# Gated linear attention and a mixer block on one core: the up product as three float32r products of 12-bit halves, with fewer buffers and a new order

## The chip, the cores and the metric

The kernel runs on one core of a Trainium2 chip. The metric is the device time of one execution in microseconds (us), the median of the runs shown. TensorE (PE) multiplies, with its weight loads shown apart as PEld; VectorE (DVE) and ScalarE (ACT) do everything between the products; GpSimd (POOL) and SyncE (SP) mostly issue transfers.

## The reference

An attention block with a complex gate feeds a mixer block. Four batches, eight heads, 768 steps, head size 48, so a model width of 384; the mixer widens to 1536.

```python
# attention, per batch and head: a complex state S (48 x 48)
mag = sqrt(a_re**2 + a_im**2); scale = minimum(mag, 0.999) / (mag + 1e-6)
for t in range(768):
    S = (a_re + 1j*a_im)[t, :, None] * scale * S + outer(k[t], v[t])
    y[t] = q[t] @ S.real
# mixer, per batch, x of 768 x 384 (heads side by side)
u = x + ((x.T @ U) @ V).T            # U: 768 x 32, V: 32 x 768
out = u + maximum(u @ w_ch1, 0.0) @ w_ch2   # 384 x 1536, 1536 x 384
```

All is float32, apart from U, V, w_ch1 and w_ch2, which arrive as float64.

## The kernel before

**Tiling.** Time is cut into 24 chunks of 128 steps, six a batch. Attention goes chunk by chunk: `gates` (L651) makes magnitudes and angles for groups of two chunks, `prep` (L849) weighs q and k and transposes them, `chain` (L883) forms the products inside the chunk and carries the 48x48 states. The mixer goes by pairs of chunks: 12 pairs, m = 0 to 11, three a batch. It can begin only when a batch's six chunks are through, because `rank` (L992, matmuls on L995) sums over all 768 steps. Then, per pair: `spread` (L1028) and `mixed` (L1041) make u from x, `turned` (L1046) transposes it into uT, an up product gives h = max(u w1, 0) in 12 blocks of 128 rows, and a down product (`down` for pair 0, `down_two` for pairs 1 to 8, `down_three` for 9 to 11; matmuls on L1270, L1313 and L1484) brings it back to 384 columns. Results leave from `leave` and `out_at`.

**The up product.** Pair 0 is multiplied ahead of its batch's rank term and corrected later. Pair 1 uses `up` (L1067): 36 float32 matmuls 128x128x256 (L1074). Pairs 2 to 11 use `up_fewer` (L1130): the 3x3 by 3x2 block product by 15 block products instead of 18. `combine` (L1221, its sums on L1234) forms eight mixed blocks of w1 once, at pair 2; `put` (L1152, sums on L1153) forms twelve mixed blocks of uT in nine DVE instructions a pair; `chain` inside it (L1174) runs 15 steps of four float32 matmuls 128x128x128 (L1181), and each step's result is copied (six times, ACT, L1189) or added on (nine times, DVE, L1193 or the helper `add`, L465). A float32 matmul shows as two records, a float32r one as one.

**Buffers.** The uT tile has two buffers, h one. QKC (weighed q or k) has three, QK (transposed q and k) three, AT two, GM two. `gate` holds six planes: x, y and two each of the real and imaginary gate. `extra` holds h of pair 0 and later mixed blocks. VP holds three chunks of v. `stage` takes the raw float64 weights, which `single` (L583) turns into float32 in w1 and w2.

**Order.** Nothing is issued as the code stands. Each operation is added to a plan with an engine, a cost, and what it reads, writes and takes: `PE`, `ACT`, `DVE`, `POOL`, `SP` (L434 to L446). Operations are numbered as they are added. `Plan.order` (L152) then issues them in the sequence of the long constant `ORDER`, checking only that needs and buffers allow it; since each engine runs its instructions in the sequence in which they are issued, `ORDER` is the schedule of every engine and queue. `SPARE` puts idle matmuls in front of a few operations to keep TensorE's clock up. Most work goes through small helpers, so that many groups of the profile share a line: `mul` (L462), `add` (L465), `act` (L459), `bounded` (L468).

float32r is already in use: from group 3 on, `split` (L732) cuts the gate's logarithms into a float32r part and a remainder, and `within` and `angles` (L747, L811) multiply each by the prefix matrix, two float32r matmuls with 384 columns a chunk:

```python
for u in range(2):
    nc.tensor.matmul(out=get(*ps), lhsT=prefix_r, rhs=of(("gs%d" % u, g), i), start=(u == 0), stop=(u == 1))
```

Of the kernel before, what the change touches and what calls it, by code (L numbers as in the profile page):

```python
# [24 lines left out]
GC = 2  # L25
# [91 lines left out]
)  # L117

SPARE = {
    122: 2, 132: 10, 193: 14, 217: 5,  # L120
}

DUMP = None
# [195 lines left out]
def kernel(  # L319
# [230 lines left out]
    for n in range(3):  # L550
        VP.append(singles.tile([128, H, D], FP, name="VP%d" % n))
# [1156 lines left out]
```

## Time and profile before

| | |
|---|---|
| median of three runs | 535.81 us (535.58 to 535.88) |
| span of the profiled execution | 533.9 us (a time of its own beside the span isn't recorded for it) |
| PE busy / PEld busy | 514.2 us (96%) / 468.1 us (88%) |
| DVE busy | 438.2 us (82%), 863 instructions |
| ACT busy | 295.8 us (55%), 531 instructions |
| POOL busy | 30.5 us (6%) |
| moved by DMA | 39.95 MB, mostly in the first half |
| granted TensorE clock | full |

How to read it: the span runs from the first to the last instruction of the program; the median also holds what lies around it. A busy share is an average over stages. PE's busy time takes in the modelled ends of pipelined matmuls, so that short gaps vanish in it. In a group's row stand line, engine, operation, out<-in, shape and count, then the busy time of the group and the mean of one in ns, then the idle time in front of it with what ended it. In the chain of waits a row is a start in us, a length in us, and what ran.

### The profile page before, as it was taken

The numbers are of one execution on the slowest core, as the hardware profiler recorded it, in microseconds if no ns is written. First come the engines' busy times: TensorE is split into PE (matmuls) and PEld (weight loads), VectorE is DVE, ScalarE is ACT, GpSimd is POOL, SyncE is SP. The second block draws the span as 40 slices with busy tenths as digits, with TensorE's granted clock in tenths as the row PEclk, the third lists the DMA queues.
The fourth block names the chain that finished last, engine by engine and source line by source line (L and its number), as shares of the span: only waits on it lengthen the run. The fifth ranks groups of instructions, "written<-read, shape, count | busy, mean of one in ns | idle before, by whom it ended". The sixth has DMA issues, their size and how long they took to land.

```text
span 533.9 us, 17164 instructions
## 1 busy us (share of the span) xinstructions
PE 514.2 (96%) x7494; PEld 468.1 (88%) x7494; DVE 438.2 (82%) x863; ACT 295.8 (55%) x531; POOL 30.5 (6%) x58
## 2 busy tenths in 40 slices
PE   2899999999999999999999999999999999999996
PEld 1777786757989989999999999999999999999996
DVE  7898988999999998897886887786878866877842
ACT  5889998893776866546647655543555412221000
POOL 1000000001020001001100001100010000000010
PEclk9999999999999999999999999999999999999999
DMA  9967985565233423601534150500240000000002
GB/s 226 206 114 194 191 145 163 171 107 112 41 75 92 63 46 80 111 1 29 118 53 83 33 106 25 98 9 23 47 70 26 2 2 1 1 2 1 1 28 97
DMA packets 150706, 39.95 MB, mean 75 GB/s; under 512 B 145880, under 2 KB 147440, under 8 KB 150624
## 3 DMA queue, kind: packets, MB, share of 16 engines
q1 hardware_dynamic: 148544, 34.63, 32.3%
q0 software_dynamic: 2080, 4.15, 2.3%
q8 instruction: 61, 1.00, 0.8%
q14 instruction: 21, 0.17, 0.1%
HBM read 33.60 MB, written 4.76 MB: 72 GB/s over the span
## 4 chain that ended last, share of the span: by engine, by line
PE 81%; DVE 11%; ACT 3%; issue 2%; DMA 2%; SPq 0%; DVEq 0%; ACTq 0%
PE down L1313 20%; PE few L1181 13%; PE bank L1181 12%; PE bank L1484 7%; PE bank L872 4%; PE bank L901 4%; PE up L1074 3%; PE bank L959 3%; PE bank L921 3%; PE bank L951 2%; DVE QKC L462 2%; PE bank L1036 1%; PE bank L747 1%; PE bank L751 1%; PE bank L811 1%
## 5 line engine op out<-in xcount | busy, mean ns | idle before, releaser
L878 ACT COPY QK<-bank 112x512 f32<-112x512 f32 x96 | 51.8, 591 | 18.2 <-PE bank L872 17.9
L1313 PE MATMUL down<-w,h 128*128 128x192 f32 x288 | 53.6, 331 | 0.0
L462 DVE TENSOR_TENSOR QKC<-qk,cs 128x768 f32<-128x768 f32 x48 | 45.0, 951 | 4.9 <-ACT cs L459 4.7
L459 ACT ACTIVATE gate<-gate 128x768 f32<-128x768 f32 (+1 forms) x50 | 39.8, 798 | 16.3 <-DVE wide L719 12.7
L1313 PEld LDWEIGHTS down<-w,h 128*128 128x128 f32 x288 | 47.0, 190 | 0.9
L465 DVE TENSOR_TENSOR xo<-bank,xo 128x192 f32<-128x192 f32 x78 | 25.3, 350 | 24.9 <-PE bank L1484 16.0
L1189 ACT COPY h<-few 128x512 f32<-128x512 f32 x35 | 20.3, 585 | 30.0 <-PE few L1181 29.9
L1074 PE MATMUL up<-uT,w 128*128 128x256 f32 x144 | 34.0, 385 | 0.2
L456 ACT ACT_TABLE_LOAD x24 | 30.8, 1283 | 1.1 <-PEq L1692 0.7
L1074 PEld LDWEIGHTS up<-uT,w 128*128 128x128 f32 x144 | 26.6, 190 | 5.0 <-DVE xo L465 0.5
L1181 PE MATMUL bank<-extra,w 128*128 128x128 f32 x232 | 30.3, 276 | 0.0
L872 PE MATMUL bank<-ident,QKC 64*112 64x64 f32 x768 | 29.1, 221 | 1.0 <-DVE G L468 0.4
L872 PEld LDWEIGHTS bank<-ident,QKC 64*112 64x112 f32 x768 | 24.4, 130 | 6.2 <-DVE QKC L462 1.4
L459 ACT ACTIVATE es<-bank 128x384 f32<-128x384 f32 x48 | 20.3, 495 | 16.6 <-PE bank L747 15.8
L797 POOL DMA_DIRECT2D gate<-F x15 | 12.5, 832 | 285.2 <-DVE F L820 167.2
L1181 PEld LDWEIGHTS bank<-extra,w 128*128 128x128 f32 x232 | 28.3, 192 | 0.1
L1313 PE MATMUL down<-stage 128*128 128x192 f32 x144 | 28.0, 332 | 0.2 <-DVE xo L465 0.2
L465 DVE TENSOR_TENSOR xo<-down,xo 128x192 f32<-128x192 f32 (+1 forms) x58 | 22.0, 386 | 7.1 <-PE down L1313 6.9
L901 PE MATMUL bank<-QK 112*64 112x64 f32 x768 | 26.6, 224 | 0.0
L901 PEld LDWEIGHTS bank<-QK 112*64 112x64 f32 x768 | 24.2, 138 | 1.3 <-issue 0.5
L459 ACT ACTIVATE cs<-F 128x384 f32<-128x384 f32 x48 | 23.3, 516 | 3.0 <-DVE F L820 2.9
L1313 PEld LDWEIGHTS down<-stage 128*128 128x128 f32 x144 | 23.5, 190 | 1.2 <-DVE xo L465 0.5
(249 smaller groups left out, 1228.6 us busy)
## 6 DMA issues: line engine op xcount, KB each, us to landing
stage<-in_moe_w_ch_dram SPq DMA_DIRECT2D x12, 768.0 KB
gate<-in_a_re_dram SPq DMA_DIRECT2D x24, 192.0 KB
gate<-in_a_im_dram SPq DMA_DIRECT2D x24, 192.0 KB
qk<-in_q_dram SPq DMA_DIRECT2D x24, 192.0 KB
qk<-in_k_dram SPq DMA_DIRECT2D x24, 192.0 KB
VP<-in_v_dram SPq DMA_DIRECT2D x24, 192.0 KB
out_dram<-xo POOLq DMA_DIRECT2D x13, 192.0 KB, 2.9
out_dram<-xo POOLq DMA_DIRECT2D x16, 96.0 KB, 2.5
```

The source lines that it names most:

```text
L456: ACT(1.4, rank, lambda: nc.scalar.preload_act_table_set(name), writes=[TABLE])
L459: return nc.scalar.activation(out=o, in_=i, func=f, **kw)
L462: nc.vector.tensor_tensor(out=o, in0=a, in1=b, op=OP.mult)
L465: nc.vector.tensor_tensor(out=o, in0=a, in1=b, op=OP.add)
L872: nc.tensor.transpose(out=get(*ps[r])[0:DQ, h], in_=get(*qkc)[at, h].rearrange("p u d -> p (u d)")[:, 0:DQ], identity=ident[at, at], tile_ ...
L878: nc.scalar.copy(out=get(*QK)[0:DQ, u].rearrange("p (h t) -> p h t", t=CH)[:, :, r * HC:(r + 1) * HC], in_=get(*ps[r])[0:DQ])
L901: nc.tensor.matmul(out=get(*ps0)[r:r + HC, h], lhsT=k_of(h, r, HC), rhs=q_of(h, r, HC), start=True, stop=True, tile_position=(0, r))
L1074: nc.tensor.matmul(out=get(*ps)[:, e], lhsT=w1[:, f, (ff + e) * 128:(ff + e + 1) * 128], rhs=get(*uT)[:, f], start=(f == 0), stop=(f == KD ...
L1181: nc.tensor.matmul(out=get(*ps)[:, q], lhsT=w()[:, q * 128:(q + 1) * 128], rhs=v[0](), start=(n == 0 and q == 0), stop=True, skip_group_ch ...
L1189: ACT(c_act(n3 * CH) - 0.045, RU, lambda i=i, k=k: nc.scalar.copy(out=at(i, k), in_=get(*ps)), [ps], [o])
L1313: nc.tensor.matmul(out=get(*to)[:, part], lhsT=x(j), rhs=y[:, j], start=(first and j == 0), stop=(j == KH - 1), skip_group_check=not first)
L1484: nc.tensor.matmul(out=get(*ps), lhsT=w[0]()[:, q], rhs=x[0]()[:, q], start=(n == 0 and q == 0), stop=(q == k3 - 1), skip_group_check=True)
```

## The change

The up product of pairs 1 to 11 becomes three float32r products. Each value is cut at a bit mask (0xFFFFF000) into a high part and a remainder. With wh, uh the high parts, wl the remainder of w1 times 2^12, ul the remainder of u, wd = wl - wh and ud = uh/2^12 - ul, the product is (wh uh + wl ul)(1 + 2^-12) + wd ud. The first two sum in one PSUM bank, the third goes to another; ACT copies the first with the factor, DVE adds the third and clips at zero. `up_fewer`, `combine` and their helpers go. Pair 0 keeps its float32 product.

```diff
+def cut_weights():                     # once, at pair 1
+    for f in range(KD):                # KD = 3
+        for y in range(2):             # halves of 768 columns
+            DVE: t  = w1 & CUT
+            DVE: w1 = w1 - t           # in place
+            ACT: wl = w1 * SHIFT       # float32r
+            DVE: wd = wl - t           # float32r
+        for y in range(2):
+            ACT: wh = copy of t        # float32r, in w1's place
```

That is the function with its arguments left out; the parts for each pair are in the kernel's own words:

```diff
@@ turned(), pairs 1 to 11
+            for r in range(2):
+                DVE(c_one(MC * KD * HC), R0, lambda r=r: nc.vector.tensor_scalar(
+                    out=top.bitcast(U32), in0=get(*tr[r]).bitcast(U32), scalar1=CUT, scalar2=None, op0=OP.bitwise_and), [tr[r]], [("low", 0)])
+                ACT(c_act(MC * KD * HC) - 0.045, R0, lambda r=r: nc.scalar.copy(out=half(get(*uh), r), in_=mixed_of(top)), [("low", 0)], [uh + (r,)])
+                DVE(c_dve(MC * KD * HC), R0, lambda r=r: nc.vector.tensor_tensor(
+                    out=half(get(*ul), r), in0=mixed_of(get(*tr[r])), in1=half(get(*uh).bitcast(FP), r), op=OP.subtract), [tr[r], uh + (r,)], [ul + (r,)])
+            DVE(c_dve(KD * N), R0, lambda: nc.vector.scalar_tensor_tensor(
+                out=get(*ud), in0=get(*uh).bitcast(FP), scalar=1.0 / SHIFT, in1=get(*ul).bitcast(FP), op0=OP.mult, op1=OP.subtract), [uh, ul], [ud])
@@ up_cut(ff), six times a pair
+            def sums(e):
+                for f in range(KD):
+                    nc.tensor.matmul(out=get(*X)[:, e], lhsT=get("wh", f)[:, at(e)], rhs=get(*uh)[:, f], start=(f == 0), stop=False)
+                for f in range(KD):
+                    nc.tensor.matmul(out=get(*X)[:, e], lhsT=wl_of(f)[:, at(e)], rhs=get(*ul)[:, f], start=False, stop=(f == KD - 1))
+            def crosses():
+                for e in range(2):
+                    for f in range(KD):
+                        nc.tensor.matmul(out=get(*Y)[:, e], lhsT=wd[:, f, at(e)], rhs=get(*ud)[:, f], start=(f == 0), stop=(f == KD - 1))
...
+            ACT(c_act(2 * N) - 0.045, R0, lambda: act(where_(), get(*X), AF.Copy, scale=1.0 + 1.0 / SHIFT), [X], [part] + own)
+            DVE(c_dve(2 * N), R0, lambda: nc.vector._custom_dve(
+                dve_ops.TENSOR_ADD_SAT, out=where_(), in0=get(*Y), in1=where_(), s0=math.inf, s1=0.0), [Y, part], done)
@@ buffers
-    w1 = singles.tile([128, KD, FF], FP, name="w1")
+    wd = singles.tile([128, KD, FF], FR, name="wd")
+    wl = singles.tile([128, KD - 1, FF], FR, name="wl")
+    for f in range(KD):
+        buffer(("w1", f), "w1_%d" % f, 1, [128, FF])
-    GL = [singles.tile([128, GC * DM], FP, name="GL")]
-    GS = [[singles.tile([128, GC * DM], FR, name="GS%d" % n)] for n in range(2)]
+    GS = [[singles.tile([128, GC * DM], FR, name="GS0")]]
-    GATE = singles.tile([128, 6, GC * DM], FP, name="gate")
+    GATE = singles.tile([128, 3, GC * DM], FP, name="gate")
-    extra = singles.tile([128, 2 * FF3 + 2 * H * CH], FP, name="extra")
+    NQ, NA, NM, NK = 2, 1, 1, 2
@@ squares of group 0's first chunk
-            ACT(c_act(2 * W) + 0.04, R1, squares, AR + AI, [X] + Y)
+            ACT(ca, R1, lambda: act(t(x), t(ar), AF.Square), AR, [X])
+            DVE(cd, R1, lambda: mul(t(y), t(ai), t(ai)), AI, Y)
@@ ORDER
-    91, 93, 95, 99, 96, 97, 101, 92, 112, 94, 113, 114, 98, 102, 103, 115, 116, 117, 0, 104, 105, 118, 119, 120, 3, 109, 110, 106, 121, 111, 107, 122,
+    92, 113, 95, 114, 115, 2206, 94, 116, 0, 93, 91, 3, 96, 97, 117, 98, 99, 5, 1, 11, 189, 190, 213, 2, 214, 147, 148, 118, 4, 102, 103, 104, 100,
...
```

So QKC has two buffers instead of three (NQ), AT one instead of two (NA), GM one instead of two (NM), QK two instead of three (NK). The second gate planes live in a pool of two planes whose place the third row block of wl (`wl2`) takes once groups 0 to 2 are done. y, the remainder of the split magnitudes and the scaled angle share one buffer; the split angle's remainder shares GL. uh, ul and ud of a pair take the three buffers of the uT tag, so one pair's halves stand there at a time. h of pair 0 goes to the h buffer. For pairs 10 and 11, thirds of h that found place in the third QK buffer go to the values' tile and to `stage`. `ORDER` is made anew in all its 2208 operations (2207 before), and `SPARE` follows the new numbers.

More of the change, by code (lines that the diff above doesn't have):

```diff
@@ L681, in magnitudes_of @@
                 return
-            def squares():
-                at, n = slice((lo - first) * DM, (hi - first) * DM), 4 if g < SINGLE and g % 2 else 2
-                act(GATE[:, 0:2, at], GATE[:, n:n + 2, at], AF.Square)
-            ACT(c_act(2 * W) + 0.04, R1, squares, AR + AI, [X] + Y)
+            ACT(ca, R1, lambda: act(t(x), t(ar), AF.Square), AR, [X])
+            DVE(cd, R1, lambda: mul(t(y), t(ai), t(ai)), AI, Y)
             DVE(cd, R1, lambda: nc.vector._custom_dve(dve_ops.TENSOR_ADD_SAT, out=t(l), in0=t(x), in1=t(y), s0=M2HI, s1=M2LO), [X] + Y, [L])
@@ L733, in split @@
             if g in SPLIT:
-                for u in range(2):
-                    ring(("gs%d" % u, g), "gs%d" % u, GS[u])
+                ring(("gs0", g), "gs0", GS[0])
+                buffer(("gs1", g), "gy", 1, [128, GC * DM], dtype=FR)
                 a, b = ("gs0", g), ("gs1", g)
@@ L841, in gates, with wl2 @@
         return magnitudes, totals, turns, waves
+    def wl2():
+        if ("wl2",) not in T:
+            T["wl2",] = pools["second"].tile([128, FF], FR, tag="second", name="wl2")
+        return T["wl2",]
     def T_of(i):
@@ L983, in out_of @@
         def out_of(nm, k, shape, padded):
-            late = nm == "uTp" and i0 >= (B - 1) * NCH + MC
-            psum((nm, k), "M" if nm in ("up", "down") or late or (nm, k) == ("rank", 0) else "T", shape, padded)
+            psum((nm, k), "M" if nm in ("up", "down") or (nm, k) == ("rank", 0) else "T", shape, padded)
             return nm, k
@@ L1037, in products @@
                                          rhs=get(*r)[at], start=True, stop=True, tile_position=(n * R, 0))
-            PE(0.45, R0, products, [r, ("V", 0)] + [uT + ("kept",)] * (m >= AHEAD), ps, way=4, steps=4 * NP)
+            PE(0.45, R0, products, [r, ("V", 0)], ps, way=4, steps=4 * NP)
             return ps
@@ L1057, in turned, with keep @@
             PE(0.39, R0, turn, us, tr, way=5, steps=2 * KD * MC)
-            for r in range(2):
-                def keep(copy, r=r):
-                    copy(out=get(*uT).rearrange("p f (c s t) -> p s c f t", c=MC, t=HC)[:, r],
-                         in_=get(*tr[r]).rearrange("p (c f) t -> p c f t", c=MC))
-                if r:
-                    ACT(c_act(MC * KD * HC) - 0.045, R0, lambda keep=keep: keep(nc.scalar.copy), [tr[r]], [uT + (r,)])
-                else:
-                    DVE(c_dve(MC * KD * HC), R0, lambda keep=keep: keep(nc.vector.tensor_copy), [tr[r]], [uT + (r,)])
+            if ahead:
+                for r in range(2):
+                    def keep(copy, r=r):
+                        copy(out=get(*uT).rearrange("p f (c s t) -> p s c f t", c=MC, t=HC)[:, r],
+                             in_=get(*tr[r]).rearrange("p (c f) t -> p c f t", c=MC))
+                    if r:
+                        ACT(c_act(MC * KD * HC) - 0.045, R0, lambda keep=keep: keep(nc.scalar.copy), [tr[r]], [uT + (r,)])
+                    else:
+                        DVE(c_dve(MC * KD * HC), R0, lambda keep=keep: keep(nc.vector.tensor_copy), [tr[r]], [uT + (r,)])
+                return
@@ new lines, in turned, with wl_of @@
+            DVE(c_dve(KD * N), R0, lambda: nc.vector.scalar_tensor_tensor(
+                out=get(*ud), in0=get(*uh).bitcast(FP), scalar=1.0 / SHIFT, in1=get(*ul).bitcast(FP), op0=OP.mult, op1=OP.subtract), [uh, ul], [ud])
+        def wl_of(f):
+            return wl[:, f] if f < KD - 1 else wl2()
+        def cut_weights():
+            for f in range(KD):
+                for y in range(2):
+                    at, t = slice(y * WP, (y + 1) * WP), ("wt", (f, y))
+                    w, l_, d_ = ("w1", f, y * WP), ("wl", f, y) if f < KD - 1 else ("wl2", y), ("wd", f, y)
+                    t_of = lambda t=t: get(*t).rearrange("p f t -> p (f t)")
+                    w_of = lambda f=f, at=at: get("w1", f)[:, at]
+                    DVE(c_one(WP), ("cut", f), lambda t_of=t_of, w_of=w_of: nc.vector.tensor_scalar(
+                        out=t_of().bitcast(U32), in0=w_of().bitcast(U32), scalar1=CUT, scalar2=None, op0=OP.bitwise_and), [w], [t])
+                    DVE(c_dve(WP), ("cut", f), lambda t_of=t_of, w_of=w_of: nc.vector.tensor_tensor(
+                        out=w_of(), in0=w_of(), in1=t_of(), op=OP.subtract), [t], [w])
+                    ACT(c_act(WP), ("cut", f), lambda f=f, at=at, w_of=w_of: act(wl_of(f)[:, at], w_of(), AF.Copy, scale=SHIFT), [w], [l_],
+                        takes=[("wl2", 0), ("wl2", 1)] if f == KD - 1 else [])
+                    DVE(c_dve(WP), ("cut", f), lambda f=f, at=at, t_of=t_of: nc.vector.tensor_tensor(
+                        out=wd[:, f, at], in0=wl_of(f)[:, at].bitcast(FP), in1=t_of(), op=OP.subtract), [l_, t], [d_])
+                buffer(("wh", f), "w1_%d" % f, 1, [128, FF], dtype=FR)
+                for y in range(2):
+                    at, t = slice(y * WP, (y + 1) * WP), ("wt", (f, y))
+                    t_of = lambda t=t: get(*t).rearrange("p f t -> p (f t)")
+                    ACT(c_act(WP), ("cut", f), lambda f=f, at=at, t_of=t_of: nc.scalar.copy(out=get("wh", f)[:, at], in_=t_of()), [t], [("wh", f, y)])
@@ new lines, in up_cut @@
+        def up_cut(ff):
+            X, Y, y = out_of("up", (m, ff), [128, 2, N], None), ("upd", (m, ff)), ff * 128 // WP
+            psum(Y, "T", [128, 2, N])
+            at = lambda e: slice((ff + e) * 128, (ff + e + 1) * 128)
+            uh, ul, ud = ("uh", m), ("ul", m), ("ud", m)
+            def sums(e):
[5 more added lines that the diff above has]
+                for e in range(2):
+                    for f in range(KD):
+                        nc.tensor.matmul(out=get(*Y)[:, e], lhsT=wd[:, f, at(e)], rhs=get(*ud)[:, f], start=(f == 0), stop=(f == KD - 1))
+            low_w = [("wl", f, y) for f in range(KD - 1)] + [("wl2", y)]
+            j = ff // k3
+            to = h if m <= THREE else third(m, j)
+            part = h + (ff,) if m <= THREE else to + ((j, "part", ff),)
+            done = [part] if m < THREE else [third_of(m, j, c) for c in range(MC)] + [part]
+            where_ = lambda: get(*h)[:, ff:ff + 2] if m <= THREE else whole_third(m, j)[:, ff % k3:ff % k3 + 2]
+            own = [] if m <= THREE or to[0] == "hq" else [("VP", n) for n in range(NT - 3, NT)] if to[1] == 4 else [
+                ("w2s", 0), ("s1", 0), ("s2", 0)]
+            for e in range(2):
+                PE(0.655, RM, lambda e=e: sums(e), [uh, ul] + [("wh", f, y) for f in range(KD)] + low_w, [X + (e,)],
+                   takes=[to] if to in plan.tag else [], steps=2 * KD)
+            PE(0.655, RM, crosses, [ud] + [("wd", f, y) for f in range(KD)], [Y], steps=2 * KD)
+            ACT(c_act(2 * N) - 0.045, R0, lambda: act(where_(), get(*X), AF.Copy, scale=1.0 + 1.0 / SHIFT), [X], [part] + own)
+            DVE(c_dve(2 * N), R0, lambda: nc.vector._custom_dve(
+                dve_ops.TENSOR_ADD_SAT, out=where_(), in0=get(*Y), in1=where_(), s0=math.inf, s1=0.0), [Y, part], done)
@@ L1073, in products @@
                     for f in range(KD):
-                        nc.tensor.matmul(out=get(*ps)[:, e], lhsT=w1[:, f, (ff + e) * 128:(ff + e + 1) * 128],
+                        nc.tensor.matmul(out=get(*ps)[:, e], lhsT=get("w1", f)[:, (ff + e) * 128:(ff + e + 1) * 128],
                                          rhs=get(*uT)[:, f], start=(f == 0), stop=(f == KD - 1))
@@ L1367, in flat_of @@
                 return parts[2][:, 0:k3 * DH].rearrange("p (j m) -> p j m", m=DH)
-            a = get("w2x", n)
+            a = F if n == 7 else get("w2x", n)
             if len(a.shape) == 3:
@@ L1426, in a @@
                 return (lambda: third_at(n, j, k)), [third_of(n, j, k)]
+            if t:
+                for n in range(2):
+                    buffer(("wk", n), "w1_%d" % n, 1, [128, FF])
             kept = [("hc", (t, n)) for n in range(8)]
+            for n, z in enumerate((1, 2, 4, 5, 6, 7)):
+                kept[z] = ("wk", n // 3, n % 3) if t else kept[z]
             def c_at(n):
@@ L1524, in mixer @@
             turned()
-        if m < AHEAD:
-            pass
-        elif m >= FEWER:
-            up_fewer()
-        else:
+        if m >= AHEAD:
+            if m == AHEAD:
+                cut_weights()
             for ff in range(0, KF, 2):
-                up(ff)
+                up_cut(ff)
         if m < PLAIN:
```

216 lines of the change are left out of this document (68 added, 148 removed), and 168 rows, old and new, of the table ORDER.

## The prediction

> **What bounds the kernel now.** I read the page's first part (busy time of each engine), then its fourth (the chain that ended last), then the windows view over three stretches.
>
> ```profile
> PE 514.2 (96%) x7494; PEld 468.1 (88%) x7494; DVE 438.2 (82%) x863; ACT 295.8 (55%) x531; POOL 30.5 (6%) x58
> ...
> PE 81%; DVE 11%; ACT 3%; issue 2%; DMA 2%; SPq 0%; DVEq 0%; ACTq 0%
> ```
>
> ```profile
> 13.00:201.00 188.00, 183.81 (x2990) 150.60 (x2988) 174.78 (x306) 150.40 (x262) 7.84 (x11) 1.00 0.58 122
> 201.00:447.00 246.00, 245.62 (x3861) 234.99 (x3861) 199.26 (x412) 127.27 (x238) 17.53 (x27) 1.00 0.26 50
> 447.00:530.00 83.00, 81.94 (x640) 80.46 (x638) 54.76 (x117) 10.73 (x19) 3.21 (x6) 1.00 0.06 19
> ```
>
> The columns are the stretch, its length, then busy time of PE, its weight loads, DVE, ACT and POOL, the granted clock (full, 1.00, throughout) and the DMA share. A busy PE overstates its work, because the ends of matmuls are modelled; the weight loads tell better. Up to 201 us they fill 150.6 of 188 us, and DVE fills 174.8: there DVE is the fullest engine and PE has gaps. From 201 us on they fill 235 of 246 and 80.5 of 83 us, DVE only 199 of 246: there PE alone is the bound. The chain of waits puts a border at 201.08 us: the product that gathers batch 1 (rank, L995) ends the wait for that batch's six chunks.
>
> ```profile
> 92.08 2.59 PE up L1074 x12
> ...
> 121.11 1.73 DVE QKC L462 x2
> ...
> 201.08 1.13 PE bank L995 x48
> ...
> 453.09 7.39 PE bank L1181 x64
> ```
>
> So I treat two stages apart: **stage A**, up to 201 us, in which the change counts by DVE work, and **stage B**, the 332.8 us from there to the span's end at 533.9, in which it counts by PE work. The span is 1.9 us under the median of the runs (535.81), and I add that at the end.
>
> **Stage B: the up product of pairs 3 to 11.** Before, a pair takes 15 products of four 128x128x128 matmuls, each two records: 120 records. After, it takes 36 blocks times three float32r matmuls of 256 columns: 108, one record each if they run like the float32r matmuls that the kernel has already. What does each cost? The chain shows trains without a gap:
>
> ```profile
> 243.02 0.35 PE bank L747 x2
> 243.38 0.97 PE down L1313 x6
> ...
> 245.24 0.36 PE bank L747 x2
> ...
> 250.14 0.89 PE few L1181 x8
> ...
> 258.45 0.36 PE bank L811 x2
> 258.81 1.96 PE few L1181 x16
> ```
>
> ```profile
> L747 PE MATMUL bank<-GS,prefix_r x36: 332/339/474, 82.4 to 374.8; 128*128 128x384 f32 x36
> L747 PEld LDWEIGHTS bank<-GS,prefix_r x36: 186/190/192, 82.4 to 374.6; 128*128 128x128 f32 x36
> ```
>
> ```profile
> L1181 PEld LDWEIGHTS bank<-extra,w 128*128 128x128 f32 x232 | 28.3, 192 | 0.1
> ```
>
> L747 and L811 are float32r. At L747 nine groups, two chunks, two halves make 36 matmuls, and there are 36 records, so each passes its columns through once. Its weight load (190 ns in the middle) looks like a float32 one (192 at L1181). A float32 record passes its columns twice. So an L1181 record moves 2x128 = 256 columns in 0.89/8 = 0.1115 us, as many as a new matmul with as large a load: the nearest row. An L1313 record moves 2x192 = 384 columns in 0.97/6 = 0.162, but a float32r one with 384 columns takes 0.35/2 to 0.36/2 = 0.175 to 0.18: 0.013 to 0.018 more for the same columns. Whether this excess goes with the columns or with the instruction, no row tells, for all float32r matmuls here have 384. By columns, 0.175x256/384 = 0.117. By instruction, 0.1115+0.0125 = 0.124. From below, two thirds of L1313's 0.162 give 0.108. I take **0.114**, between the equal row and the share by columns; the ends 0.108 and 0.124 stay for the range.
>
> Per pair: 120x0.1115 = 13.4 us before, 108x0.114 = 12.3 after. Nine pairs: 9x(13.38-12.31) = **-9.6 us**. At 0.108 it is -15.5, at 0.1115 -12.0, at 0.117 -6.7, at 0.124 +0.1.
>
> A rule on this: the Trainium skill, "TensorE: Matmul & The Clock Gate", section "Back-to-back issue gap", gives N/2.4 + 2.5 ns for a warm matmul, by which, as an estimate, 256 columns cost 0.109 us, and stage B would give 9x(13.38-11.77) = -14.5; by that rule the whole comes to 526.7. By that rule 384 columns cost 0.1625: the trace agrees for float32 (0.162) and not for float32r (0.175 and more).
>
> **What else the change puts on the engines.** Rows (mean ns of one):
>
> ```profile
> L617 DVE TENSOR_SCALAR w<-w 128x768 uint32<-128x768 uint32 x12 | 6.6, 556 | 0.5 <-ACT w L459 0.3
> L738 DVE TENSOR_TENSOR GS<-GL,GS 128x768 fp32r<-128x768 f32 x9 | 8.6, 955 | 0.3
> L462 DVE TENSOR_TENSOR QKC<-qk,cs 128x768 f32<-128x768 f32 x48 | 45.0, 951 | 4.9 <-ACT cs L459 4.7
> L1060 DVE COPY uT<-bank 128x384 f32<-128x384 f32 x10 | 5.5, 549 | 1.6 <-PE bank L1055 1.6
> L806 DVE TENSOR_TENSOR GS<-gate,GS 128x384 fp32r<-128x384 f32 x18 | 10.0, 554 | 0.3
> L1193 DVE CUSTOM_DVE_ANT_1 h<-few,h 128x512 f32<-128x512 f32 x28 | 18.9, 684 | 3.8 <-PE few L1181 3.5
> L459 ACT ACTIVATE gate<-gate 128x768 f32<-128x768 f32 x43 | 36.3, 843 | 16.1 <-DVE wide L719 12.5 <-DMA gate<-in_a_im_dram 2.9
> L1060 ACT COPY uT<-bank 128x384 f32<-128x384 f32 x10 | 4.8, 484 | 16.7 <-PE bank L1055 16.6
> ```
>
> ```profile
> sum 534.00, DVE 27.80; mean DVE 9.27
> ...
> sum 534.00, DVE 8.88; mean DVE 2.96
> ```
>
> The last two are the windows view of L1153 (the 90 sums of u, 9 a pair) and of L1234 (the 13 sums of combine). Neighbours on DVE overlap: two of 0.951 (L462) take 1.73 in the chain, so each is worth 0.086 less than its row.
>
> - Cutting w1, once: six pieces, each an AND (0.556) and two subtractions (0.955): 6x(2.466-0.258) = +13.2 us of DVE, and twelve ACT copies of 0.843, 10 us on an engine with 150.4 of stage A's 188 us filled. The AND of u reads PSUM, so I price it as L1060's copy (0.549).
> - combine goes: 8.88-13x0.086 = -7.8.
> - A pair by the new way: two ANDs, two subtractions (0.554), one of 768 (0.955), six saturating sums (0.684): 7.27-11x0.086 = 6.3. By the old way: 2.78 of sums of u, nine of 0.684, one copy: 9.5-19x0.086 = 7.9. Pair 1 had only the copy (0.46): +5.9. Each later pair: -1.5.
> - Group 0's squares: one moves from ACT to DVE, +0.5.
>
> **Stage A.** Up to the rank of batch 1 that is 13.2+5.9-7.8-1.5+0.5 = +10.3 us of DVE, all on the engine that bounds this stage. But the order is new: I numbered the operations of both versions as the code adds them and walked both lists, adding these rows. At the rank of batch 1 DVE has 178.0 us behind it in the old list and 182.2 in the new one, so 6.1 us of other DVE work now stands later, where DVE has room. PE has 161.7 and 156.1, ACT 150.8 and 153.9: no other engine takes over. I take **+4.2 us**; the bounds are 0 (DVE's gaps, 13 of the 188 us, swallow it) and +10.3 (the move frees nothing). Behind the mark, 1.2 us of other products are added to PE: **+1.2**.
>
> In stage B the u cuts and the sums lie beside PE: before pairs 10 and 11 the new list has three or four cross products (0.7 us each) between the last product that reads the old halves and the first that needs the new ones, and the copies, AND and subtraction behind it take 0.484+0.549+0.484+0.554 = 2.1 us and their hand-offs. If that cover fails, up to 2.1 us a pair are exposed. The queues of SP and POOL get no new transfer. The single AT, GM and the two QKC and QK buffers add waits for attention's next chunk: nothing by my count, since down products stand between; the price without cover is a rival below.
>
> **Sum.** 535.8 + 4.2 - 9.6 + 1.2 = 531.6; I say **531.5 us**, with 529.5 to 535 for 0.112 to 0.1175 a matmul.
>
> **Rivals.**
> 1. *float32r costs no more than its columns* (0.108 to 0.112): 525.7 to 529.7. For it: L1181's and L1313's rows, where columns alone set the pace. Against it: every float32r train above. The Trainium skill's rule above falls in this case.
> 2. *The excess sits in each instruction* (0.1175 to 0.124): 535 to 541, the case on the other side. For it: 0.175 against 0.162 with equal columns, and it is the same whether L1313 (243.38) or L1181 (258.81) follows. It decides from 0.118 us a matmul, where 9x(13.38-108c) falls to the 5.4 us that the other terms add.
> 3. *The cut starves stage A.*
>
> ```profile
> 85.30:131.80 46.50, 19.74 (x84) 15.46 (x84) 1.00 0.56 131
> ```
>
> This is the windows view of the up product (L1074) alone: its 84 records between 85 and 132 us, 72 of pair 1 (15.5 us at 2.59/12 a record), needed nothing from DVE but one copy and filled PE while DVE worked. Now pair 1 waits for the whole cut; in the new list its first product stands behind 105.5 us of DVE instead of 73.0. Each of the six pieces goes DVE, ACT, DVE; if DVE idles for each copy (0.843), stage A costs 5.1 us more: 537, and up to 547 if PE never makes up the 15.5 us of filler. Against it: the new list has other work between those steps.
> 4. *Fewer buffers starve attention*: AT is read by the next chunk's PE pass, QKC by the transposes and the state product. If 18 chunks each expose half a microsecond, +9: up to 541. Against it: the down and up products still fill PE.
>
> That the matmuls aren't single-pass is excluded by L747's count.
>
> **Chances.** Forecast 0.36 (faster 0.33, same 0.03); rival 1 0.22, all faster; rival 2 0.20 (same 0.06, slower 0.14); rival 3 0.14 (same 0.02, slower 0.12); rival 4 0.08 (faster 0.03, same 0.01, slower 0.04). Same means within 0.2%, about what a measurement can tell from no change. Together: faster 0.58, same 0.12, slower 0.30. The range reaches from rival 1's bottom with stage A at its lower bound (522) to rival 2's top (541); rival 3's tail stays out.
>
> **What would show it.** Right: the new up products in trains of six at 0.67 to 0.70 us; L995's second pass near 205 us; PE full behind it; DVE some 5 us less busy in all. Wrong: trains of 0.73 (rival 2) or under 0.67 (rival 1); PE idle between 90 and 130 us before pair 1's up product (rival 3); waits of the AT or QKC lines on products behind 201 us (rival 4).

## The result, and the profile after

The kernel after takes 540.76 us (median of five runs, 537.87 to 542.13), the kernel before 535.80 beside it: ratio 1.0089, interval 1.0066 to 1.0112. It is slower, where 531.5 us and a gain were forecast; the time lies just inside the range of 522 to 541, at its top. The profiled execution took 541.01 us with a span of 539.1.

The busy time of each engine, and the granted clock in 40 slices (tenths of full speed):

```profile
PE 512.4 (95%) x7410; PEld 469.0 (87%) x7410; DVE 430.7 (80%) x798; ACT 311.0 (58%) x554; POOL 30.0 (6%) x57
...
PEclk9979998799999999999999999999999999999997
```

DVE has 7.5 us less to do, and ACT 15 more. The clock, which was full before, dips three times in the first 110 us. The windows view over the three stretches shown of before (length; busy PE, PEld, DVE, ACT, POOL; clock; DMA share and rate):

```profile
13.00:201.00 188.00, 179.34 (x2855) 148.59 (x2855) 171.01 (x291) 152.50 (x259) 7.72 (x11) 0.95 0.61 122
206.00:447.00 241.00, 240.97 (x3784) 230.50 (x3783) 190.27 (x356) 136.79 (x254) 17.87 (x28) 1.00 0.27 51
447.00:530.00 83.00, 81.83 (x624) 80.86 (x622) 55.05 (x113) 12.24 (x23) 2.68 (x5) 1.00 0.05 19
```

From 206 us on TensorE is as full as before. The chain of waits gives the borders (start, length, what ran); first before, then after. L995 is the rank product before and L1003 after, L1484 and L1463 are the last down products, L1155 a train of new up products:

```profile
201.08 1.13 PE bank L995 x48
...
518.22 10.74 PE bank L1484 x64
```

```profile
206.26 1.13 PE bank L1003 x48
...
459.13 2.87 PE bank L1155 x24
...
488.43 39.07 PE bank L1463 x240
```

The difference of the spans, 5.2 us, splits at these borders. **Stage A** (to the rank product of batch 1) is 5.2 longer. **Stage B** to the end of the last down product takes 321.2 us (527.50 less 206.26) instead of 327.9: 6.7 shorter. **The tail** behind the last down product takes 11.6 us (539.1 less 527.50) instead of 4.9: 6.7 longer. The tail was not in the prediction at all.

### The profile page after: what moved, and what is told of

Read it like the earlier page. It is cut to its first block, busy times and chain, and to the rows that moved or that the text cites. A ratio compares the mean times of both kernels' runs of the same rounds, so it can differ in the third digit from the quotient of the medians.

```text
span 539.1 us, 16918 instructions
## 1 busy us (share of the span) xinstructions
PE 512.4 (95%) x7410; PEld 469.0 (87%) x7410; DVE 430.7 (80%) x798; ACT 311.0 (58%) x554; POOL 30.0 (6%) x57
## 4 chain that ended last, share of the span: by engine, by line
PE 84%; DVE 7%; ACT 5%; issue 1%; ACTq 0%
PE down L1286 21%; PE up L1148 9%; PE bank L1155 9%; PE up L1150 9%; PE bank L1463 7%; PE bank L881 4%; PE bank L910 4%; PE bank L968 4%; PE bank L930 3%; PE bank L960 3%; PE up L1179 1%; PE bank L814 1%; PE bank L1063 1%; PE bank L750 1%; PE bank L754 1%
## 5 line engine op out<-in xcount | busy, mean ns | idle before, releaser
L1148 PE MATMUL up<-uh,wh 128*128 128x256 f32 x396 | 71.0, 288 | 0.7 <-DVE xo L467 0.7
L1150 PE MATMUL up<-ul,wl 128*128 128x256 f32 x396 | 68.6, 282 | 0.0
L461 ACT ACTIVATE h<-up 128x512 f32<-128x512 f32 x60 | 35.5, 595 | 42.1 <-PE up L1150 42.1
L1148 PEld LDWEIGHTS up<-uh,wh 128*128 128x128 f32 x396 | 56.8, 189 | 1.9 <-DVE xo L467 0.9
L1150 PEld LDWEIGHTS up<-ul,wl 128*128 128x128 f32 x396 | 56.2, 189 | 0.0
L1155 PE MATMUL bank<-ud,wd 128*128 128x256 f32 x396 | 54.9, 282 | 0.0
L1155 PEld LDWEIGHTS bank<-ud,wd 128*128 128x128 f32 x396 | 50.6, 188 | 0.1
L1169 DVE CUSTOM_DVE_ANT_0 h<-bank,h 128x512 f32<-128x512 f32 x54 | 35.7, 687 | 14.1 <-PE bank L1155 12.2
L1286 PE MATMUL down<-stage 128*128 128x192 f32 x192 | 35.5, 333 | 0.0
L800 POOL DMA_DIRECT2D z<-F x15 | 12.2, 810 | 337.5 <-DVE F L823 133.4
```

Source lines behind the costliest of these rows:

```text
L461: return nc.scalar.activation(out=o, in_=i, func=f, **kw)
L1148: nc.tensor.matmul(out=get(*X)[:, e], lhsT=get("wh", f)[:, at(e)], rhs=get(*uh)[:, f], start=(f == 0), stop=False)
L1150: nc.tensor.matmul(out=get(*X)[:, e], lhsT=wl_of(f)[:, at(e)], rhs=get(*ul)[:, f], start=False, stop=(f == KD - 1))
L1155: nc.tensor.matmul(out=get(*Y)[:, e], lhsT=wd[:, f, at(e)], rhs=get(*ud)[:, f], start=(f == 0), stop=(f == KD - 1))
L1169: DVE(c_dve(2 * N), R0, lambda: nc.vector._custom_dve(dve_ops.TENSOR_ADD_SAT, out=where_(), in0=get(*Y), in1=where_(), s0=math.inf, s1=0.0 ...
L1286: nc.tensor.matmul(out=get(*to)[:, part], lhsT=x(j), rhs=y[:, j], start=(first and j == 0), stop=(j == KH - 1), skip_group_check=not first)
```

## The experiments: the tail

The timeline of the last microseconds of after:

```profile
527.33 1.28 PE L1605 MATMUL warm<-ident 128*128 128x128 f32 x10
...
528.44 0.54 POOL L1450 DMA_DIRECT2D out_dram<-xo  x1 [3.06 <-issue]
...
528.87 0.15 DVE L1595 CAST flag<-bank 1x1 int32<-1x1 f32 x1 [0.92 <-PE bank L1593]
```

`judge`, which counts what the fast path can't do and writes a flag that every engine loads before the final branch, stands last in the new order; so does an output issued by POOL. The view of the closing lines shows what POOL does then, first of before, then of after (count; shortest, middle and longest in ns; first and last start). A drain of 3.73 us is POOL's, and its start is the first of the two times:

```profile
L1703 POOLq DRAIN  x3: 46/112/3728, 527.9 to 533.6; - x3
```

```profile
L1681 POOLq DRAIN  x3: 46/112/3729, 534.5 to 538.8; - x3
```

Before, that drain begins 1.1 us ahead of the end of the last products (528.96); in after it begins 7.0 us behind it (527.50). What POOL's sequencer did ahead of it, in after:

```profile
L1636 POOLq EVENT_SEMAPHORE  x5: 17/43/753, 529.7 to 530.7; - x5
L1636 POOLq COMPARE_BRANCH  x2: 38/39/40, 529.6 to 531.9; - x2
L1636 POOLq INC_SWDGE_SEM  x1: 1063/1063/1063, 530.8 to 530.8; - x1
```

It branches on the flag at 529.6, waits until 530.8 for its own outputs to land, and the span ends 8.3 us later. Two things are late, flag and output, and the experiments take them one by one.

**flag_early**: the end of `judge` moved ahead in the order.

```diff
-    ... 2096, 2203, 2201, 2098 ...   ... 2086, 2202, 2207, 2104, 2204, 2205,
+    ... 2096, 2203, 2201, 2202, 2204, 2205, 2098 ...   ... 2086, 2207, 2104,
-        psum(ps, "T", [128, 1], [128, 512])
+        psum(ps, "M", [128, 1], [128, 512])
```

> The kernel after, with the judge's last three operations (the limit on least, the count on PE, the flag on DVE) moved from the very end of the order to some 15 us before it, and its PSUM bank taken from the other ring; warm and the outputs stay. Theory (the tail grew because POOL begins its closing steps late: it needs both the flag and the landing of its own last output, which is issued at 528.4 us): no gain worth naming, 540.8 less 0 to 0.6 us, because POOL's output still goes out at 528.4 and its 3.73 us drain still begins near 534. Rival (the flag alone is late): about 5 us less, 535.5. Rival (the end is not tied to either; the loss lies in clock and products): 540.8, with the drain in the same place.

Measured: 542.45 us (541.53 to 544.68). The flag is written at 512.9, but POOL comes to load it only behind its own output, issued at 526.95. The flag alone gives nothing, as the theory has it. But the time is 1.7 us above that of after, where 0 to 0.6 less was expected: POOL waits until 531.4 for that output to land, though it was issued 1.5 us sooner than in after (where the wait ends at 530.8). Why it lands later isn't shown.

**out_sp** and **flag_out**: an output given to SP, without and with the early flag.

```diff
-                if t:
+                if t or i == 1:
                     SP(0.6, ("load", 0), lambda: f(nc.sync), [o], [("out", n)])
```

> The kernel after, with the one last output of chunks 18 to 20 that POOL issues at 528.4 us given to SP instead; the judge stays last. Theory (POOL needs both): POOL's part waits for no transfer of its own any more, but for the flag at 529.0; its branch then runs about 1 us sooner, so 539.8 (540.8 less 0.7 to 1.3). Rival (POOL's last output alone is late): about 5 us less, 535.5. Rival (neither): 540.8.

> Both of the edits before. Theory (POOL needs both): POOL reads the flag near 515 us, its drain of 3.73 us runs beside the last products, and from the last sum to the end it takes 4.6 us as in the kernel before, not 10.1: 535.6 (534.8 to 536.5), the median of the kernel before. Rival (neither; the loss lies elsewhere): 540.8.

Measured: 539.46 (537.83 to 541.46) and 542.84 us (540.79 to 544.80). Both are misses of mine: the edit moved the output of chunk 19, and the one issued last is that of chunk 20, whose sum by product E stands last. In both profiles POOL still issues an output behind the last down product. They say nothing on the theory: that out_sp comes close to the expected 539.8 is chance, and flag_out lies 7 us above its 535.6.

**flag_out20**: flag_early with `t or i == 2`.

> The kernel after with the judge moved ahead as in flag_early, and the output that POOL really issues last (chunk 20, whose sum by product E stands last in the order; out_sp and flag_out had moved that of chunk 19) given to SP. Theory (POOL closes late because both its flag and its last output are late): from the last matmul of the products to the end 5 to 6 us instead of 10, POOL's drain of 3.73 us beside the last products; 535.7 (534.5 to 537), the rest of the spread being the clock in the first 110 us. Rival (neither is the cause): 540.8 and the drain still behind the last product.

Measured: 538.43 us (537.13 to 540.25), less than half of the gain. Now the last of POOL's outputs stands behind that of chunk 19 at 523.94 and goes out at 525.53; POOL's last wait ends at 528.2, and the span of 536.7 ends 8.5 us later.

**flag_outall**: flag_early with all three outputs of chunks 18 to 20 on SP (`if t >= 0`).

> The kernel after with the judge moved ahead as in flag_early, and all three outputs of chunks 18 to 20 given to SP, so that POOL keeps only the outputs of pair 8, which are ready earlier. Theory (the span ends 8.3 to 8.7 us after POOL's last wait, for flag or output, as in every profile so far: 530.7 and 539.1 after, 531.3 and 539.7 in flag_early, 528.1 and 536.7 in flag_out20): POOL's last wait comes before 520 us, its drain runs beside the products, and SP's last output sets the end, 4.6 us behind the last sum as before: 535.7 (534 to 537.5). Rival (flag_out20 has taken all that is to be had there): 538.4.

Measured: 535.54 us (533.85 to 538.23, 12 runs), ratio to before 1.0002 (0.9984 to 1.0020). Its closing lines:

```profile
L1681 POOLq DRAIN  x3: 46/112/3483, 519.3 to 533.0; - x3
```

The drain begins at 519.3, beside the products. Against after's 540.76 that is 5.2 us, as much as after had lost against before (5.0).

**before_flag_late**: the reverse, in the kernel before.

```diff
-    ... 2178, 2093, 2203, 2160, 2176, 2173, 2181, 2204, ... 2195, 2196,
+    ... 2178, 2093, 2160, 2176, 2173, 2181, ... 2195, 2196, 2203, 2204,
```

> The kernel before, with the judge's count and flag moved to the very end of its order; nothing else. Theory: POOL's drain comes out from under the last products, and the time grows by 4 to 5 us, from 535.8 to about 540.3. Rival (the end is not tied to the flag): 535.8 to 536.2.

Measured: 540.93 us (540.58 to 541.40), ratio 1.0106 (1.0091 to 1.0120). Two operations that together last half a microsecond cost 5.4 us by their place alone:

```profile
L1703 POOLq DRAIN  x3: 46/112/3728, 534.1 to 538.4; - x3
```

So either one is enough to make the end late: the output in flag_early, the flag here.

## The experiments: the price of a float32r matmul

**trains**: trains of 60 matmuls on 128 rows, each form on a line of its own (L38 and L54 float32 with 128 columns, L56 with 256; float32r with 128, 192, 256, 384 and 512 columns on L40 to L48; L50 256 columns with 64 weight columns; L52 256 with the same weights throughout; L58 bfloat16 with 256).

> No part of the reference: trains of 60 matmuls of 128 rows, each form on a line of its own, to price a float32r matmul by itself. Theory (the excess over its columns sits in each float32r instruction): 256 columns 0.117 to 0.120 us, 128 columns 0.064 to 0.067, 384 columns 0.172 to 0.176, 512 columns 0.225 to 0.229, all about 0.012 over columns/2.4 GHz, the scale at which a pass of 128 float32 columns took 0.0557. Rival (it goes with the columns): 128 columns 0.059, 512 columns 0.235. Rival (it is the weight load): 64 weight columns or the same weights again bring 256 columns down to 0.107 to 0.110. float32 and bfloat16 stay within 0.003 of their columns.

The chain of its profile (start, length, line, records):

```profile
20.18 6.65 PE bank L40 x60
26.84 6.73 PE bank L42 x60
33.57 7.22 PE bank L44 x60
40.79 10.40 PE bank L46 x60
51.20 13.64 PE bank L48 x60
64.84 6.81 PE bank L50 x60
71.64 7.20 PE bank L52 x60
78.84 13.40 PE bank L54 x120
92.24 25.90 PE bank L56 x120
118.15 6.55 PE bank L58 x60
```

256 columns take 7.22/60 = 0.120 us, 384 take 0.173, 512 take 0.227: 0.107 for the last 256 columns, so about 0.013 of each matmul is not columns. The first theory holds there. It fails at 128 columns: 0.111, not 0.065, and 192 columns cost 0.112 too. So does a float32 record (L54), which passes 256 columns; half of L56's 0.216 would be 0.108. By these numbers something else sets the pace below some 235 columns, an estimate: there 0.013 and the columns come to the floor's 0.1115. The same weights again (L52) change nothing; half as many weight columns (L50) give 0.1135 and so halve the excess. So the rival that blames the weight load holds in part; what the excess is stays open. float32 with 256 columns takes 0.216 a record, for 512 columns passed, and bfloat16 0.109.

**no_low**: one of the three products left out.

```diff
-                for f in range(KD):
-                    nc.tensor.matmul(out=get(*X)[:, e], lhsT=wl_of(f)[:, at(e)], rhs=get(*ul)[:, f], start=False, stop=(f == KD - 1))
```

> The kernel after without the products of the low halves (wl by ul): 36 of the 108 float32r matmuls of each of the pairs 1 to 11 are left out, the cuts stay. Theory (from 105 us on TensorE sets the pace and each such matmul costs 0.1185 us in place): 11 times 36 times 0.1185 is 46.9, less what DVE takes over: 494 to 500 us. Rival (something else shares the bound, DVE at 80% above all): 505 or more.

Measured: 521.21 us (519.48 to 524.84), 19.6 less than after where 41 to 47 were expected: the theory fails, and the rival's bound holds. From the rank product of batch 1 to the last down product it is 16.6 us faster than after (201.28 to 505.87), for 9x36 matmuls worth 38.7 at 0.1195. The waits of TensorE from 206 us on (in all, times, longest):

```profile
PE up L1148 <- ACT h L461: 2.7, 4, 0.8
...
PE bank L1463 <- DVE hq L1169: 1.5, 1, 1.5
PE up L1148 <- ACT uh L1106: 1.3, 1, 1.3
PE bank L881 <- DVE h L1169: 0.8, 1, 0.8
PE bank L1155 <- DVE ud L1109: 0.7, 1, 0.7
```

With the product gone TensorE waits for the copies of the sums (h) and the cuts of u behind it. All rows of this view add up to 13.6 us, of the 22.1 that are missing from the 38.7; where the rest lies isn't shown. So stage B was bound by TensorE, but with less reserve than I had thought: of a large saving there, less than half would have reached the end in this order.

## The experiments: stage A

The prediction called stage A bound by DVE. **no_wd** takes DVE work out of it.

```diff
+    nc.gpsimd.memset(wd.bitcast(FP), 0.0)
-    out=wd[:, f, at], in0=wl_of(f)[:, at].bitcast(FP), in1=t_of(), op=OP.subtract
+    out=wd[:, f, at][:, 0:8], in0=wl_of(f)[:, at].bitcast(FP)[:, 0:8], in1=t_of()[:, 0:8], op=OP.subtract
```

> The kernel after without the work of the last subtraction in the cut of w1: the six subtractions that write wd keep their place but work on 8 columns instead of 768, and POOL fills wd with zeros at the start, so the cross products multiply by zeros (left out: six times about 0.85 us of DVE). Theory (stage A, up to the rank product of batch 1, is bound by DVE): that product and the whole come 3.5 to 5 us earlier, 536.5. Rival (stage A waits for something else, clock or hand-offs between DVE and ACT): less than 1.5 us, 540.

Measured: 539.72 us (538.59 to 541.70), 1.0 less than after; in its profile, taken of the slowest of its runs, the rank product of batch 1 stands at 206.82, no earlier than in any profile of this stage A (203.2 to 206.3). The theory falls for this work: taking some 5 us of DVE out of stage A leaves its end where it was. But the work lies late. In after the six subtractions start from 101.8 us on:

```profile
L1130 DVE TENSOR_TENSOR wd<-wl,wt x6: 947/950/953, 101.8 to 121.9; 128x768 fp32r<-128x768 f32 x6
```

On DVE's work ahead of that the run says nothing. So I compared TensorE stretch by stretch (columns as above), before and then after:

```profile
25.00:60.00 35.00, 34.05 (x626) 26.91 (x622) 32.40 (x56) 31.35 (x56) 0.00 (x0) 1.00 0.74 162
60.00:85.00 25.00, 24.34 (x594) 19.37 (x592) 22.26 (x34) 22.27 (x44) 0.00 (x0) 1.00 0.82 174
85.00:105.00 20.00, 19.95 (x157) 15.17 (x154) 17.59 (x38) 17.63 (x25) 0.96 (x1) 1.00 0.54 151
105.00:206.00 101.00, 100.07 (x1575) 85.02 (x1575) 96.14 (x174) 72.77 (x130) 6.88 (x10) 1.00 0.40 78
```

```profile
25.00:60.00 35.00, 30.97 (x599) 23.91 (x598) 32.26 (x54) 30.00 (x54) 0.00 (x0) 0.90 0.90 191
60.00:85.00 25.00, 24.15 (x533) 20.10 (x532) 24.09 (x42) 24.85 (x42) 0.00 (x0) 1.00 0.83 198
85.00:105.00 20.00, 17.61 (x206) 11.29 (x202) 16.09 (x31) 15.21 (x27) 0.00 (x0) 0.74 0.67 136
105.00:206.00 101.00, 99.83 (x1570) 88.12 (x1569) 92.97 (x160) 74.95 (x130) 7.72 (x11) 1.00 0.40 70
```

From 105 us on TensorE is full in both: its waits from there to 206 us (in all, times, longest) are these, before and then after.

```profile
PE bank L747 <- DVE extra L1115: 0.5, 1, 0.5
PE down L1313 <- DVE xo L465: 0.2, 1, 0.2
```

```profile
PE up L1148 <- DVE xo L467: 0.7, 1, 0.7
PE bank L930 <- issue: 0.4, 1, 0.4
```

Ahead of it, its weight loads fill 61.5 us (26.91 + 19.37 + 15.17) before and 55.3 after, with a hole of 3 us up to 60 and one of 3.9 between 85 and 105. The new theory: what TensorE doesn't do by 105 us is paid at the end of the stage, and what is missing between 85 and 105 are pair 1's up products, which can't start before the cut. Before, they start at 91.91 us, in after here:

```profile
120.83 0.81 PE L1148 MATMUL up<-uh,wh 128*128 128x256 f32 x3
```

**before_up1_late** takes them away from the kernel before: operations 449 to 454, 459 and 460 (four of pair 1's up products and their copies), and 461 to 463, which need them, moved behind operation 458 in `ORDER`.

> The kernel before with four of pair 1's six up products (48 records of 0.216 us, 10.4 us, that run between 92 and 106 us) moved behind the other two, to about 130 us, with their copies and the two sums that need them. Theory (up to about 105 us TensorE waits for DVE and ACT and needs these products to fill it; from there on it is full, so what it doesn't do by then is paid at the rank product of batch 1 and at the end): that product at 207 to 211 us instead of 201, time 541.5 to 546. Rival (stage A is bound by DVE, as the prediction had it): that product at 201 to 203, time at most 537.5.

Measured: 547.50 us (547.32 to 548.44), ratio 1.0228 (1.0215 to 1.0242): 11.7 us for 10.4 us of products that were only moved. The rank product of batch 1 comes at 213.22 instead of 201.08. Its window between 85 and 105 us looks like that of after, clock included, though no operation of the change is in it:

```profile
85.00:105.00 20.00, 16.12 (x126) 8.93 (x128) 18.15 (x39) 16.70 (x24) 1.39 (x1) 0.83 0.55 152
```

Up to 126 us nothing is lost: TensorE comes to pair 1's last two products at 125.94 us in before and at 125.77 here, though the other four are gone from ahead of them. So there they had filled time in which TensorE would have waited. Then the moved ones follow and cost their full length (a row of before, then two of this run):

```profile
125.94 5.81 PE L1074 MATMUL up<-uT,w 128*128 128x256 f32 x24
```

```profile
125.77 5.45 PE L1074 MATMUL up<-uT,w 128*128 128x256 f32 x24
131.91 10.63 PE L1074 MATMUL up<-uT,w 128*128 128x256 f32 x48
```

This run does not tell which engine sets the pace behind 126 us, because DVE stands still meanwhile:

```profile
DVE stage L1305 <- ACT h L459: 12.2, 1, 12.2
```

An operation on h that was moved along (L1305) waits for the copies of the moved products, and all that DVE has behind it waits too; a stage bound by DVE would lose as much. The traces of before and after tell more. From the end of pair 0's down product to the rank product of batch 1 TensorE takes 76.9 us before (124.11 to 201.01) and 85.4 in after (120.83 to 206.19). Counted from the start of each record to the start of the next, the up products take 19.5 us of that before and 27.8 in after, 8.3 more; all the rest takes 0.1 more. With the 3.3 us by which after gets there sooner this makes 8.3 + 0.1 - 3.3 = 5.1, the loss of the stage (5.2) but for rounding.

**keep_warm** asks what the falling clock costs.

```diff
-    123: 2, 133: 10, 194: 14, 218: 5,
+    123: 2, 133: 10, 194: 14, 218: 5, 201: 7, 244: 7, 394: 7, 395: 4, 442: 3, 409: 2, 418: 2, 415: 2, 412: 2,
```

> The kernel after with 34 more matmuls of the identity (128x128 float32, 0.22 us each) ahead of the products that start after a gap of TensorE or among tiled products: 7 each ahead of inner product 0, up product 0.1 and the first before-product of chunk 5, 4 ahead of its inside product, 3 ahead of the spread of pair 1, 2 ahead of each of the first four corrections. Theory (the granted clock falls to a half after such gaps and that costs stage A up to 3 us): granted clock back at 0.99 to 1.00, the rank product of batch 1 at 202 to 204 us, 538 (537 to 539.5), spread of the runs under 1.5 us. Rival (the clock falls for another reason, or where TensorE isn't the bound): 540.8 or up to 3 us more for the added products, clock as before.

Measured: 544.29 us (543.35 to 546.70), slower by 3.5 than after, with a clock of 1.00 between 85 and 105 us (0.74 in after) and the rank product of batch 1 at 207.46, where 202 to 204 were expected. The added matmuls, 34 times 0.22 or 7.5 us, cost more than the clock gave; those ahead of operation 394 wrote over part of a sum.

**flag_outall_warm** does it with eight, on top of flag_outall.

```diff
+    201: 4, 409: 1, 418: 1, 415: 1, 412: 1,
```

> flag_outall with eight more matmuls of the identity (0.22 us each): four ahead of inner product 0, where TensorE waits 1.5 us at 28 us, and one ahead of each of the first four corrections (all into banks that the following product writes whole). Theory (the granted clock falls to a half at 30 to 37 and 98 to 105 us, the second costs up to 3 us): clock of both windows back at 0.95 or more, 1 to 3 us less than flag_outall. Rival (the added products cost as much as the clock gives, as in keep_warm, whose 34 took 3.5 us more though its clock was whole; there the seven ahead of the before-product of chunk 5 wrote over part of a sum): 0 to 2 us more than flag_outall.

Measured: 535.62 us (533.43 to 536.11, 12 runs), ratio to before 0.9993 (0.9982 to 1.0004). The median is that of flag_outall; what goes is the upper end of the runs, 536.1 instead of 538.2. The clock between 85 and 105 us was 0.83 in its profile, where 0.95 or more was expected. So the dips explain part of the spread of the kernel after; what they cost its median isn't shown, as the added matmuls take up to 1.8 us themselves. The profiles that share after's stage A give a hint: the rank product of batch 1 comes at 203.30 us in out_sp, whose clock was 1.00 between 85 and 105 us, at 204.50 in flag_outall and at 206.26 in after, both with 0.74. So up to 3 of after's 5.2 us may be the clock's. No version that does the whole work beats the kernel before.

**before_few** does the smaller buffers alone.

```diff
-    for n in range(3):
+    for n in range(2):
         QKC.append(...)
-    for n in range(2):
+    for n in range(1):
         AT.append(...)
-        buffer(mid_G, "GM", 2, [DQ, H, D])
+        buffer(mid_G, "GM", 1, [DQ, H, D])
```

> The kernel before with the smaller buffers of attention alone: one AT and one GM instead of two, two QKC instead of three; its order mended only where an operation would take a buffer too early (it then waits in the list until the buffer is free, which is a crude order, so a loss is an upper bound). Theory (TensorE loses its time up to 105 us for want of up products, not of buffers): at most 1 us more than before, 536 to 537, and the rank product of batch 1 at 200 to 202 us. Rival (the fewer buffers starve attention): 2 to 9 us more, 538 to 545, most of it before 70 us, where the kernel after has lost some 4 us more than the kernel before.

Measured: 601.61 us (600.82 to 604.52), 66 more, where the theory had at most 1 and the rival 2 to 9. This bounds nothing useful: at pair 1's last up products TensorE is 2.8 us behind (128.70 for 125.94), and the rest is lost later, where the mended order makes attention wait far down the list (the later rank products come at 227.84, 369.32 and 498.97). It shows that this mended order can't live with the smaller buffers; how much of the 3 us that after loses up to 60 us is theirs, and how much the new order's, stays open.

## Why the prediction was wrong, point by point

**The price of a float32r matmul** (0.114 us) was mis-sized. It measures 2.87/24 = 0.1195 in after's trains and 0.120 alone. With that a pair costs 108x0.1195 = 12.91 us and nine save 9x(13.38 - 12.91) = 4.2, not 9.6. The old price was too low as well: 0.89/8 is 0.111, and the rows shown with it have dearer trains (7.39/64 = 0.1155, 1.96/16 = 0.1225). Counted from the start of each record to the start of the next, the 1080 records of L1181 in stage B take 124.0 us before (0.1148 each), the 972 new ones 118.5 in after (0.1219 each): 5.5 us saved. This is rival 2, whose point of decision was 0.118. That its 535 to 541 holds the result is in part luck: with 5.5 in place of 9.6 the sum gives 535.7, and the 5 us from there to 540.76 are the end of the order. The row that I called the nearest, L1181's 0.1115, was no price of 256 columns: the train of float32r with 128 columns costs the same 0.111, so that row was a floor. The row that had the answer was the other one, 384 float32r columns in 0.175, read as a fixed amount in each instruction (0.013 in the trains at 256, 384 and 512 columns alike). By the rule of the Trainium skill quoted in the prediction ("TensorE: Matmul & The Clock Gate", "Back-to-back issue gap"), which that section gives for a single isolated matmul, 256 columns would, as an estimate, take 0.109: bfloat16 agrees (0.109), float32r doesn't (0.120).

**The end of the order** was not priced at all; this is the step that left out most, 5.2 us by flag_outall. I wrote that the queues of SP and POOL get no new transfer. That is true and beside the point: none is new, but one of POOL's now stands last, and so does `judge`. I had walked both orders with their operations' costs up to the rank of batch 1 and stopped there.

**Stage A** came out near its number, by another cause. Forecast +4.2; after's profile has +5.2, and those of the versions that differ from it only at the end have 203.2 to 205.4 for the rank product of batch 1, +2.2 to +4.3. The likeness is luck. The step that failed here is that DVE's sum sets the end of the stage: the 5 us of it that no_wd leaves out, from 101.8 us on, moved nothing. What is paid there, by the count over both traces, are 8.3 us of up products that no longer stand in TensorE's gaps ahead of 105 us, less 3.3: the lost filler of rival 3, with TensorE's weight loads at 11.3 of 20 us between 85 and 105. Rival 3's own price, DVE idle for each copy of the cut, isn't there: none of DVE's waits from 60 to 206 us in after names wl or wd. What holds the first 105 us back, and how much of it is the clock, stays open; before_up1_late, with its 12 us, shows what such filler is worth but not by which engine.

**Stage B** was bound by TensorE as said, and shrank by 6.7 us in the profile and 4.8 in flag_outall (204.50 to 527.63), for 8.4 forecast. Of this 5.5 are the up products'. The 1.2 us of other products that were to come behind the mark did not: outside the up and down products TensorE spends 75.8 us there in both. The cuts of u and the sums lay beside the products as said: from 206 us to the last down product no wait of TensorE is on record. Of the smaller buffers the single AT shows the sign of rival 4, on DVE alone (waits from 201 us on in after):

```profile
DVE AT L913 <- PE bank L910: 8.5, 7, 6.0
```

Before, such waits come to 0.5 us. TensorE, which sets the pace there, did not wait for them.

DVE came out 7.5 us less busy, for 5 forecast.

**Sum of the spans with the measured terms** (borders of one profile each, so that they add up by construction): 533.9 + 3.4 (rank product at 204.50) - 4.8 + 0.7 (tail 533.3 less 527.63, for 4.9) = 533.2 is flag_outall, whose profile has 533.3. For after it is 533.9 + 5.2 - 6.7 + 6.7 = 539.1.

## What to carry to other kernels

Walk a new order to its very end: what the engine with the longest closing steps waits for last is on the path, however small it is. An operation in a stage that one engine fills on average may still be needed there as filler for another; before moving it, ask what the other engine does in those microseconds, and which queue will stand behind it in its new place. And a row is a price only if the thing priced sets its pace: two shapes with one duration point to a floor.

## What the hardware showed unasked

- A float32r matmul with 128 weight columns took 0.111 us with 128 columns and 0.112 with 192; with 256, 384 and 512 it took 0.013 more than its columns (0.107 for 256), and with 256 columns and 64 weight columns 0.007 more.
- POOL's closing steps: from the end of its last wait to the end of the span 8.3 us in after (530.8 to 539.1), 8.5 in flag_out20 and 8.6 in before_flag_late, of which the drain is 3.7.
- The granted clock fell to 0.74 on average between 85 and 105 us in after, where TensorE's longest gap was 1.6 us.
